# Row maxima in wider PSUM tiles: nine max items a pair instead of twelve, and none ahead of a score stretch

## The chip, the cores and the metric

One core of a Trainium2 chip runs the whole program in one launch. The metric is device time in microseconds (us) from the first to the last instruction and what lies around it, the median of several executions. The engines are named as in the profile: PE (TensorE matmul), PEld (its weight loads), DVE (VectorE), ACT (ScalarE), POOL (GpSimd), SP (SyncE, which issues the DMAs).

## What is computed

The reference, cut to its core: attention over keys with query rows pooled in twos, a soft mixture of experts over its rows, and a gated layer.

```python
def _attn_ref(q, k, v):                      # 4 x 8 heads, 1152 keys, 64 wide
    q_pool = q.reshape(B, H, S // 2, 2, D).mean(axis=3)      # 576 query rows a head
    scores = scale * np.matmul(q_pool, k.transpose(0, 1, 3, 2))
    scores = scores - np.max(scores, axis=-1, keepdims=True)
    attn = np.exp(scores)
    attn = attn / (np.sum(attn, axis=-1, keepdims=True) + 1e-09)
    return np.matmul(attn, v)

def _moe_ref(x, phi, w1, w2):                # 2304 rows, 8 experts with 4 slots each
    logits = x @ phi
    d = np.exp(logits - logits.max(0, keepdims=True))        # over the rows
    d /= d.sum(0, keepdims=True) + 1e-09
    ...                                      # slots, experts, combination

def _moe2_ref(x, w_gate, w_val, w_out, rms_g):   # RMS norm, silu gate, product
    ...
```

The part that the change touches is `np.max(scores, axis=-1)` of the attention, and the maximum over rows in `logits.max(0)`.

## The kernel before, in words

The 32 heads are taken as 16 pairs p; the two heads of a pair stand on partitions 0 to 63 and 64 to 127. For each pair there are nine key tiles `kt` of 128 keys and two halves `h` of 288 query rows. `qk` makes the scores of one (kt, h): four products for each head, the fourth of which subtracts the row maximum (`mr`), into a PSUM tile of two banks, one a head. ACT takes the exponential of it (`e`), POOL sums the exponentials (`add_e`, L395), and `av` multiplies them with the values (L401). `av` runs at every third key tile (`VISIT`), so that a third of a pair is: a stretch of six `qk` (48 score matmuls in the trace, 24 couples of one matmul a head), then a **visit** with the products with the values and all the small steps.

The row maximum must be there before the scores of a pair begin. It is made one pair ahead: a **max item** (`max_item`) multiplies 128 query rows of both heads with 384 keys (L327), and DVE reduces both banks in one instruction (L329). Twelve items, and two tail items for the last 64 query rows of both heads (L334, L335), make a pair's maxima. Then `max_red` (L340) takes the maximum over the key blocks, `max_row` turns it on PE (`mxt`, L345) and ACT copies it negated (`mrow`), and `send_row` sends it to `mr` by DMA.

The order of the work is written out by hand. `STEP` and `STEP_V` are the steps of one key tile; `m` marks where a max item may stand, `a b c` the three `av`. `MAX` gives the number of items that each key tile adds, and `AHEAD` how many items of the pair after next are made at a pair's end. `AT` gives each side step its moment: 5.75 is in key tile 5, at three quarters of its steps. In a visit stand also `sums`, `recips` and the two tail items (visit 1, key tile 2), `x_logits` (xl, L471) with `x_share` (L480) and `logit_add` (visit 2), and `x_turn` (xo, L453) with `x_divide` (xt, L462) (visit 3). In every fourth pair, `d_turn` (lgt, L508) turns the logits of a batch in visit 3 of the pair: six transposes into a tile of two banks, three a bank, and a maximum on DVE for each bank (mm, L509).

Scores, max items, xl, xo, lgt, sums and the other small results share one ring of three PSUM tiles of two banks (`tag="u", bufs=3`); whoever wants a tile waits until the engine that reads its former content is done:

```python
    def two_banks(name):
        return ps.tile([128, 2, 512], F32, tag="u", bufs=3, name=name)
```

After the last pair come the experts (hin, so), whose weights arrive by DMA, and the gated layer (yo, gv).

Of the kernel before, what the change touches and what calls it, by code (L numbers as in the profile page):

```python
# [15 lines left out]
AX = mybir.AxisListType  # L16
# [12 lines left out]
NF = 12  # L29

STEP = "q0 m q1 m e0 e1".split()
STEP_V = "q0 q1 m e0 e1 a m m b c m".split()
STEP_0 = "q m m e a b c".split()
VISIT = 3
PART = 5
MAX = [0, 0, 4, 0, 0, 4, 0, 0, 4]
MAX_1 = [2, 2, 4, 1, 0, 4, 0, 0, 4]
AHEAD = 5
AT = dict(
    take_x=0.0,  # L40
    load_64=[0.1, 3.0, 5.0],
# [3 lines left out]
    sum_q=2.2,  # L45
    round_k=[2.5, 5.5],
    abs_64=[2.51, 8.5, 8.51],
    d_back=2.68,
    d_copy=2.69,
    sums=2.7,  # L50
    max_tail=[2.75, 2.76],
    recips=2.77,
    turn_64=[0.5, 1.0, 3.3],
    low_q=3.2,
    high_q=5.51,
    block_q=5.52,
    max_red=5.65,
    slot_part=5.66,
    slot_copy=5.67,
    x_logits=5.7,  # L60
    max_row=5.83,
    send_row=6.0,
    x_share=6.05,
    logit_add=6.06,
    low_k=[6.1, 7.2],
    load_v=7.3,
    d_turn=8.66,
    slot_turn=8.67,
    x_turn=8.7,
    x_divide=[8.71, 8.72],  # L70
    drop_x=8.73,
    d_exp=8.85,
    c_soft=[3.5, 5.53, 8.96],
    load_ew=[1.0, 3.4],
# [39 lines left out]
    slot_part_a=8.2,  # L114
    slot_turn_a=9.43,
)
MAX_0 = [2, 1, 1, 1, 1, 1, 1, 1, 1, 1, 1, 2, 1, 1, 1, 1, 1, 0]
HALVED = (0, 15)
SQ_DVE = (0, 2)
SP_ACT = (1, 5, 4, 3, 2)  # L120
# [28 lines left out]
def attention_softmoe_gated_kernel(ctx: ExitStack, tc: tile.TileContext, kT, qT, vv, ip, cst, w1, w2, wg, wv, wo, rg, out):  # L149
# [78 lines left out]
    def two_banks(name):  # L228
        return ps.tile([128, 2, 512], F32, tag="u", bufs=3, name=name)
# [88 lines left out]
    def max_item(p, i):  # L318

        if i == 0:  # L320
            mx3[p] = S([128, 2 * NQT + 1, 3], "mx3")
        o = two_banks("mxp")
        if i < 12:
            t, c = divmod(i, 3)
            for s in range(2):
                r = slice(64 * s, 64 * s + 64)
                pe.matmul(o[:, s, 0:KC], lhsT=qh[p][r, 128 * t:128 * t + 128], rhs=kh[p][r, KC * c:KC * c + KC], start=True, stop=True)  # L327
            to = mx3[p][:, 0:2 * NQT].rearrange("p (s t) c -> p s t c", s=2)[:, :, t, c]
            dv.reduce_max(out=to, in_=o[:, :, 0:KC], axis=AX.X)  # L329
        else:  # L330
            n = 2 if i == 12 else 1
            for j in range(n):
                c = 2 * (i - 12) + j
                pe.matmul(o[:, j, 0:KC], lhsT=tb, rhs=kh[p][:, KC * c:KC * c + KC], start=True, stop=True)  # L334
            dv.reduce_max(out=mx3[p][:, 2 * NQT, 2 * (i - 12):2 * (i - 12) + n], in_=o[:, 0:n, 0:KC], axis=AX.X)  # L335

    rows = {}

# [160 lines left out]
    def d_turn(g):  # L499

        b, hs = groups[g]
        mm = S([32, 2], "mm")
        both = two_banks("lgt") if attention[0] else None
        o = []
        for i, h in enumerate(hs):
            o.append(both[0:32, i, 0:HQ] if attention[0] else bank([32, HQ], "lgt"))
            for t in range(3):
                pe.transpose(out=o[i][:, TB * t:TB * t + TB], in_=lg[b][:, 3 * h + t, :], identity=ident[0:TB, 0:TB])  # L508
            dv.reduce_max(out=mm[:, i:i + 1] if len(hs) > 1 else mall[:, g:g + 1], in_=o[i], axis=AX.X)  # L509
        if len(hs) > 1:  # L510
            dv.reduce_max(out=mall[:, g:g + 1], in_=mm, axis=AX.X)
        return o

    def d_neg(g):
# [177 lines left out]
    def side(p):  # L692
        n, m, l = p + 1, p + 2, p - 1
        todo = []

        def at(name, g):
            ts = (AT_0 if p == 0 else AT_15 if p == NP - 1 else AT).get(name, AT.get(name))
            for i, t in enumerate(ts if isinstance(ts, list) else [ts]):
                todo.append((t, len(todo), (lambda i=i: g(i))))

        if p == 0:
            at("round_k1", lambda i: round_k(1, i))
            at("block_q1", lambda i: block_q(1))
        if n < NP:
            at("low_k", lambda i: low_k(n, slice(576 * i, 576 * i + 576)))
            at("low_q", lambda i: low_q(n))
            at("load_v", lambda i: load_v(n))
            if p:
                at("max_tail", lambda i: max_item(n, 12 + i))
            at("max_red", lambda i: max_red(n))  # L710
            at("max_row", lambda i: max_row(n))
            at("send_row", lambda i: send_row(n))
        if m < NP:
            at("load_q", lambda i: load_q(m))
            at("load_k", lambda i: load_k(m))
            at("sum_q", lambda i: sum_q(m))
            at("high_q", lambda i: high_q(m))
            at("block_q", lambda i: block_q(m))
            at("round_k", lambda i: round_k(m, i))
        if l >= 0:  # L720
            at("take_x", lambda i: take_x(l))
            at("sums", lambda i: sums(l))
            at("recips", lambda i: recips(l))
            at("x_turn", lambda i: x_turn(l, range(3 * i, 3 * i + 3)) if p == NP - 1 else x_turn_all(l))
            at("x_divide", lambda i: x_divide(l, range(3 * i, 3 * i + 3)))
            at("drop_x", lambda i: rel("B"))
            at("x_logits", lambda i: x_logits(l, range(6)))
            at("x_share", lambda i: x_share(l, range(6)))
            at("logit_add", lambda i: logit_add(l))
            if p % 4 == 0 and p < NP - 1:  # L730
                at("d_turn", lambda i: dpart.__setitem__(("d", l // 4), (d_turn(l // 4), d_neg(l // 4))))
                at("d_exp", lambda i: d_exp(l // 4, *dpart.pop(("d", l // 4))))
            if p % 4 == 1 and p > 1:
                b = p // 4 - 1
                at("d_back", lambda i: d_back(b))
                at("d_copy", lambda i: d_copy(b))
                at("slot_part", lambda i: slot_part(b))
                at("slot_copy", lambda i: slot_copy(b))
                at("slot_turn", lambda i: slot_turn(b, pt[:, b]))
            if p % 4 == 2 and p > 2:  # L740
                b = p // 4 - 1
                at("c_soft", lambda i: (c_max, c_exp, c_soft2)[i](b))
        if 0 < p < NP - 2:
            at("load_64", lambda i: load_64() if i < 2 or p % 2 or p < 8 else None)
            at("load_ew", lambda i: load(1, 99, KEEP_C + min(len(doubles), 4 * HELD + HELD_O)) if p >= FIRST_EW else None)
        if p < NP - 1:
            at("spill", lambda i: spill())
            at("abs_64", lambda i: abs_64(1))
            at("turn_64", lambda i: turn_64(1))
        if p == NP - 2:  # L750
            spill()
            assert not doubles
            at("load_14", lambda i: (keep_b.__setitem__(0, KEEP[3]), load(1, KEEP_A[0])))
        if p == NP - 1:
            at("take_x_a", lambda i: take_x(p, (0,)))
            at("sums_a", lambda i: sums(p, (0,)))
            at("recips_a", lambda i: recips(p, (0,)))
            at("x_turn_a", lambda i: x_turn(p, ((0, 1), (2,))[i]))
            at("x_divide_a", lambda i: x_divide(p, ((0, 1), (2,))[i]))
            at("x_logits_a", lambda i: (x_logits(p, range(3)), x_share(p, range(3))))  # L760
            at("logit_add_a", lambda i: logit_add(p, (0,)))
            at("d_exp_a", lambda i: d_exp(3, d_turn(3), d_neg(3)))
            at("d_back_a", lambda i: (d_back(3), d_copy(3)))
            at("slot_part_a", lambda i: (slot_part(3), slot_copy(3)))
            at("slot_turn_a", lambda i: slot_turn(3, pt[:, 3]))
            at("load_15", lambda i: (keep_b.__setitem__(0, KEEP[0]), load(1, KEEP_A[1])))
        return sorted(todo, key=lambda x: x[:2])

    with tc.manual_schedule():
# [47 lines left out]
        def next_max(p, mx):  # L817
            if p == 0:
                mx += 9
                if mx < 14:  # L820
                    max_item(0, mx)
                    if mx == 13:
                        max_red(0)
                        max_row(0)
                        send_row(0, 3)
                else:
                    max_item(1, mx - 14)
            elif p == 1:
                max_item(2 + mx // 12, mx % 12)
            else:  # L830
                mx += AHEAD
                max_item(p + 1 + mx // 12, mx % 12)

        for p in range(NP):
            todo = side(p)
# [2 lines left out]
            for u, (kt, h) in enumerate(steps):  # L838
                now = u / 2 if p in HALVED else u
                order = STEP_0 if h is not None else STEP_V if kt % VISIT == VISIT - 1 else STEP  # L840
                quota = min(sum((MAX_0 if p == 0 else MAX_1 if p == 1 else MAX)[:u + 1]),
                            0 if p == NP - 1 else 12 - AHEAD if p == NP - 2 else 99)
                for i, step in enumerate(order):
                    while todo and todo[0][0] <= now + i / len(order) / len(steps) * 9:
                        todo.pop(0)[2]()
# [426 lines left out]
```

## Time and profile before

| | |
|---|---|
| time of three runs | 764.63, 765.6 and 769.43 us, median 765.6 |
| the profiled execution | 768.76 us, its span 766.7 us |
| PE busy | 726.6 us, 95% of the span |
| DVE, ACT, POOL busy | 61%, 52%, 59% |
| mean granted clock of TensorE | 0.987 |

The attention takes the first 510 us or so. Busy shares are averages over stages, and ends of matmuls are modelled, so that a busy PE may still lose time between matmuls; the starts of one stretch and of the next show it better.

### The profile page before, as it was taken

How to read it: one execution, taken by the hardware profiler on the slowest of the kernel's cores; microseconds unless marked ns; L12 is line 12 of the kernel's file. 1: busy time of each engine (PE TensorE's matmuls, PEld its weight loads, DVE VectorE, ACT ScalarE, POOL GpSimd, SP SyncE). 2: the span in 40 equal slices, each digit the busy share in tenths (PEclk: the TensorE clock that was granted, in tenths of full speed). 3: DMA queues.
4: the chain of work that ended last, by engine and by line, in shares of the span. 5: the costliest groups of instructions: out<-in, count | busy, mean ns of one | idle time of the engine just before them, and what ended most of it. 6: DMA issues, size and time to landing. Idle time of an engine off the chain costs nothing.

```text
span 766.7 us, 15557 instructions
## 1 busy us (share of the span) xinstructions
PE 726.6 (95%) x6143; PEld 503.5 (66%) x6143; DVE 468.0 (61%) x711; ACT 396.1 (52%) x809; POOL 448.5 (59%) x340
## 2 busy tenths in 40 slices
PE   4989999989999998999998999979989999999998
PEld 2556666656666665666666566644437788888887
DVE  5867877876688876678876665343134665545420
ACT  2455665655655654565565454343227775555330
POOL 5336887966768876778796577213005765535330
PEclk9999999999999999999999999997999999999999
DMA  4231452653625625445335053248994010000001
GB/s 168 93 110 54 174 177 88 226 190 125 215 95 208 212 74 204 141 145 191 127 132 199 6 169 125 100 165 311 377 382 167 1 56 28 15 27 29 29 27 42
DMA packets 52856, 103.57 MB, mean 135 GB/s; under 512 B 5816, under 2 KB 19632, under 8 KB 52784
## 3 DMA queue, kind: packets, MB, share of 16 engines
q1 hardware_dynamic: 52784, 102.59, 38.1%
q8 instruction: 48, 0.79, 0.4%
q14 instruction: 24, 0.20, 0.1%
HBM read 89.39 MB, written 13.11 MB: 134 GB/s over the span
## 4 chain that ended last, share of the span: by engine, by line
PE 82%; DVE 9%; ACT 4%; DMA 3%; issue 2%; POOL 1%; SPq 0%; ACTq 0%; DVEq 0%
PE yo L1175 19%; PE av L401 19%; PE sc L378 17%; PE mxp L327 5%; DVE mx L329 5%; PE gv L1127 3%; PE sums L421 2%; PE xl L471 2%; ACT e L380 2%; PE hin L944 2%; PE mxp L334 2%; DVE w L683 1%; PE xo L453 1%; PE so L967 1%; DMA w<-away 1%
## 5 line engine op out<-in xcount | busy, mean ns | idle before, releaser
L395 POOL TENSOR_TENSOR acc<-acc,e 128x576 f32<-128x576 f32 x148 | 215.2, 1481 | 60.9 <-ACT e L380 50.3
L380 ACT ACTIVATE e<-sc 128x576 f32<-128x576 f32 x288 | 170.2, 652 | 119.9 <-PE sc L378 118.0
L329 DVE TENSOR_REDUCE mx<-mxp 128x2 f32<-128x768 f32 x192 | 178.4, 955 | 87.7 <-PE mxp L327 86.1
L401 PE MATMUL av<-e,vt 128*64 128x288 f32 x1152 | 169.3, 425 | 0.0
L395 POOL TENSOR_TENSOR acc<-e 128x576 f32<-128x576 f32 x60 | 109.1, 1838 | 91.1 <-ACT e L380 91.1
L401 PEld LDWEIGHTS av<-e,vt 128*64 128x64 f32 x1152 | 74.5, 139 | 60.9 <-issue 26.6
L378 PE MATMUL sc<-qh,kh 64*128 64x288 f32 x576 | 95.8, 327 | 4.3 <-DVE mx L329 3.9
L1175 PE MATMUL yo<-woh,hA 128*128 128x512 f32 (+1 forms) x312 | 99.0, 384 | 0.0
L378 PE MATMUL sc<-mr,pick 64*128 64x288 f32 x576 | 86.4, 293 | 1.0 <-DMA mr<-mrow 1.0
L378 PE MATMUL sc<-qh,kl 64*128 64x288 f32 x576 | 85.9, 293 | 0.0
L378 PE MATMUL sc<-ql,kh 64*128 64x288 f32 x576 | 85.7, 292 | 0.0
L1132 DVE SCALAR_TENSOR_TENSOR th<-th,gv 128x384 f32<-128x384 f32 x72 | 39.9, 554 | 62.8 <-ACT th L1129 62.4
L327 PE MATMUL mxp<-kh,qh 64*128 64x384 f32 x384 | 70.7, 401 | 7.1 <-ACT kh L794 5.8
L1158 POOL TENSOR_TENSOR hA<-hu,hA 128x384 fp32r<-128x384 f32 x48 | 48.8, 1017 | 42.6 <-ACT hA L1157 38.8
L378 PEld LDWEIGHTS sc<-qh,kh 64*128 64x128 f32 x576 | 54.8, 185 | 27.5 <-DVE mx L329 16.2
L1175 PEld LDWEIGHTS yo<-woh,hA 128*128 128x128 f32 x312 | 57.6, 188 | 10.2 <-issue 0.7
L327 PEld LDWEIGHTS mxp<-kh,qh 64*128 64x128 f32 x384 | 34.1, 191 | 42.9 <-ACT e L380 16.3
L1175 PE MATMUL yo<-wol,hA 128*128 128x512 f32 (+1 forms) x151 | 57.8, 383 | 0.0
L1129 ACT ACTIVATE th<-gv 128x384 f32<-128x384 f32 x72 | 35.3, 490 | 42.4 <-PE gv L1127 39.1
L378 PEld LDWEIGHTS sc<-mr,pick 64*128 64x128 f32 x576 | 55.1, 185 | 1.4 <-DMA mr<-mrow 1.4
L378 PEld LDWEIGHTS sc<-qh,kl 64*128 64x128 f32 x576 | 55.5, 187 | 0.0
L378 PEld LDWEIGHTS sc<-ql,kh 64*128 64x128 f32 x576 | 55.0, 186 | 0.0
(180 smaller groups left out, 1038.4 us busy)
## 6 DMA issues: line engine op xcount, KB each, us to landing
w<-in_w_dram SPq DMA_DIRECT2D x86, 256.0 KB
w<-in_w_dram SPq DMA_DIRECT2D x21, 512.0 KB
vt<-in_vv_dram SPq DMA_DIRECT2D x16, 576.0 KB
qraw<-in_qT_dram SPq DMA_DIRECT2D x15, 576.0 KB
kraw<-in_kT_dram SPq DMA_DIRECT2D x15, 576.0 KB
away<-w SPq DMA_DIRECT2D x32, 256.0 KB
w<-away SPq DMA_DIRECT2D x32, 256.0 KB
raw<-in_wg_dram SPq DMA_DIRECT2D x12, 512.0 KB
```

The lines of the kernel that those rows point to most:

```text
L327: pe.matmul(o[:, s, 0:KC], lhsT=qh[p][r, 128 * t:128 * t + 128], rhs=kh[p][r, KC * c:KC * c + KC], start=True, stop=True)
L329: dv.reduce_max(out=to, in_=o[:, :, 0:KC], axis=AX.X)
L334: pe.matmul(o[:, j, 0:KC], lhsT=tb, rhs=kh[p][:, KC * c:KC * c + KC], start=True, stop=True)
L378: pe.matmul(o[:, s, 0:HQ], lhsT=w[r, wk], rhs=q[r, c], start=(i == 0), stop=(i == 3))
L380: ac.activation(ets[p, kt, h], o[:, :, 0:HQ], AF.Exp, scale=0.0625)
L395: eng.tensor_tensor(out=acc[p, h, j], in0=first[p, h, j] if n == 1 else acc[p, h, j], in1=e, op=ALU.add)
L401: pe.matmul(avt[p, h][64 * s:64 * s + 64, 0:HQ], lhsT=vt[p][:, kt, 64 * s:64 * s + 64], rhs=ets[p, kt, h][:, s], start=(kt == 0), stop=(kt ...
L1127: pe.matmul(o[i], lhsT=sg[n][:, 256 * i + 128 * c:256 * i + 128 * c + 128], rhs=cT[g], start=True, stop=True)
L1129: ac.activation(t, o[0], AF.Tanh, scale=0.5)
L1132: dv.scalar_tensor_tensor(out=t, in0=t, scalar=1.0, in1=o[0], op0=ALU.add, op1=ALU.mult)
L1158: gp.tensor_tensor(out=b, in0=u, in1=f(a), op=ALU.subtract)
L1175: pe.matmul(o, lhsT=x, rhs=w[:, c], start=(ft == 0 and i == 0), stop=(ft == NF - 1 and i == 2))
```

## The change

For pair 0 all stays as it was. From pair 1 on, a max item covers 512 keys and fills both its banks (L350 and L351 of the changed kernel): eight such items for keys 0 to 1023, and a ninth (L356, L357) that takes the last 128 keys for all four blocks of 128 query rows, in eight matmuls of 128 columns, with one reduction to eight columns. The two tail items take 2 x 512 and 128 keys. `MAX`, `MAX_1`, `MAX_0` and `AHEAD` follow (three items at each visit), and the last `m` of `STEP_V`, which put an item between a visit and the next stretch of scores, is gone. In `d_turn` the maxima of both banks are taken by one instruction after all six transposes. Side steps have new moments; of these `x_share` and `logit_add` go ahead of `max_row`, and `d_back` and `d_copy` behind `recips`.

```diff
-STEP_V = "q0 q1 m e0 e1 a m m b c m".split()
+STEP_V = "q0 q1 m e0 e1 a m m b c".split()
...
-MAX = [0, 0, 4, 0, 0, 4, 0, 0, 4]
-MAX_1 = [2, 2, 4, 1, 0, 4, 0, 0, 4]
-AHEAD = 5
+MAX = [0, 0, 3, 0, 0, 3, 0, 0, 3]
+MAX_1 = [1, 1, 3, 1, 0, 3, 0, 0, 3]
+NMAX = 9
+AHEAD = 3
...
-    x_share=6.05,
-    logit_add=6.06,
+    x_share=5.785,
+    logit_add=5.79,
...
         if i == 0:
             mx3[p] = S([128, 2 * NQT + 1, 3], "mx3")
+        if p:
+            return wide_item(p, i)
         o = two_banks("mxp")
...
+    def wide_item(p, i):
+
+        o = two_banks("mxp")
+        q, k, m = qh[p], kh[p], mx3[p]
+        heads = m[:, 0:2 * NQT].rearrange("p (s t) c -> p s t c", s=2)
+        rest = slice(1024, 1152)
+        if i < 8:
+            t, c = divmod(i, 2)
+            for s in range(2):
+                r = slice(64 * s, 64 * s + 64)
+                pe.matmul(o[:, s, :], lhsT=q[r, 128 * t:128 * t + 128], rhs=k[r, 512 * c:512 * c + 512], start=True, stop=True)
+            dv.reduce_max(out=heads[:, :, t, c], in_=o, axis=AX.X)
+        elif i == 8:
+            for t in range(NQT):
+                for s in range(2):
+                    r = slice(64 * s, 64 * s + 64)
+                    pe.matmul(o[:, s, 128 * t:128 * t + 128], lhsT=q[r, 128 * t:128 * t + 128], rhs=k[r, rest], start=True, stop=True)
+            dv.reduce_max(out=heads[:, :, :, 2], in_=o.rearrange("p s (t k) -> p s t k", t=NQT), axis=AX.X)
+        elif i == 9:
+            for c in range(2):
+                pe.matmul(o[:, c, :], lhsT=tb, rhs=k[:, 512 * c:512 * c + 512], start=True, stop=True)
+            dv.reduce_max(out=m[:, 2 * NQT, 0:2], in_=o, axis=AX.X)
+        else:
+            pe.matmul(o[:, 0, 0:128], lhsT=tb, rhs=k[:, rest], start=True, stop=True)
+            dv.reduce_max(out=m[:, 2 * NQT, 2:3], in_=o[:, 0:1, 0:128], axis=AX.X)
...
-            dv.reduce_max(out=mm[:, i:i + 1] if len(hs) > 1 else mall[:, g:g + 1], in_=o[i], axis=AX.X)
         if len(hs) > 1:
+            dv.reduce_max(out=mm, in_=both[0:32, :, 0:HQ], axis=AX.X)
             dv.reduce_max(out=mall[:, g:g + 1], in_=mm, axis=AX.X)
+        else:
+            dv.reduce_max(out=mall[:, g:g + 1], in_=o[0], axis=AX.X)
```

On PE, a plain pair's visit 2 and the begin of the next stretch of scores (mxp is a max item, sc a score) read before:

```order
L327 MATMUL mxp<-kh,qh 128x384 x2
L401 MATMUL av<-e,vt 64x288 x4
L327 MATMUL mxp<-kh,qh 128x384 x4
L471 MATMUL xl<-ipt,xu 96x64 x6
L401 MATMUL av<-e,vt 64x288 x8
L345 MATMUL mxt<-cs,mxw 128x128
L327 MATMUL mxp<-kh,qh 128x384 x2
L378 MATMUL sc<-qh,kh 128x288 x2
```

The same place in the changed kernel:

```order
L350 MATMUL mxp<-kh,qh 128x512 x2
L430 MATMUL av<-e,vt 64x288 x4
L350 MATMUL mxp<-kh,qh 128x512 x2
L356 MATMUL mxp<-kh,qh 128x128 x8
L500 MATMUL xl<-ipt,xu 96x64 x6
L430 MATMUL av<-e,vt 64x288 x8
L374 MATMUL mxt<-cs,mxw 128x128
L407 MATMUL sc<-qh,kh 128x288 x2
```

The max item ahead of the scores is gone, and the third item of this visit is the one of eight short matmuls.

On DVE, the reductions of the same visit with what stands before and behind them (w is the turning of 64-bit weights, ls and lg are `x_share` and `logit_add`), before:

```order
L329 TENSOR_REDUCE mx_1248<-mxp 128x2
L307 TENSOR_TENSOR ql<-qs,qh 128x576
L683 SCALAR_TENSOR_TENSOR w_1484<-w_1484,raw_1397 128x512
L329 TENSOR_REDUCE mx_1248<-mxp 128x2 x3
L340 TENSOR_REDUCE mxw<-mx_1248 128x9
L329 TENSOR_REDUCE mx_1652<-mxp 128x2
L480 TENSOR_TENSOR ls<-xl,rr 96x384
L490 TENSOR_TENSOR lg<-lg,ls 96x192
```

The same place in the changed kernel:

```order
L308 TENSOR_TENSOR ql<-qs,qh 128x576
L714 SCALAR_TENSOR_TENSOR w_1458<-w_1458,raw_1371 128x512
L351 TENSOR_REDUCE mx_1315<-mxp 128x2 x2
L357 TENSOR_REDUCE mx_1315<-mxp 128x8
L369 TENSOR_REDUCE mxw<-mx_1315 128x9
L509 TENSOR_TENSOR ls<-xl,rr 96x384
L519 TENSOR_TENSOR lg<-lg,ls 96x192
```

A reduction is gone ahead of ql and another ahead of ls.

On DVE, the maxima of the turned logits in every fourth pair, before:

```order
L329 TENSOR_REDUCE mx_2064<-mxp 128x2 x3
L509 TENSOR_REDUCE mm<-lgt 32x1 x2
L511 TENSOR_REDUCE mall<-mm 32x1
L516 TENSOR_SCALAR nm<-mall 32x1
L462 TENSOR_TENSOR xt<-xo,rr 96x3x128 x2
```

The same place in the changed kernel:

```order
L351 TENSOR_REDUCE mx_2119<-mxp 128x2 x3
L539 TENSOR_REDUCE mm<-lgt 32x2
L540 TENSOR_REDUCE mall<-mm 32x1
L547 TENSOR_SCALAR nm<-mall 32x1
L491 TENSOR_TENSOR xt<-xo,rr 96x3x128 x2
```

Two reductions, one a bank, have become one over both banks. The orders of SP and of POOL are the same in both kernels.

## Rows read from the trace of the kernel before

**Rows 1.** The page, part 1: engine, busy us, share of the span, instructions.

```profile
PE 726.6 (95%) x6143; PEld 503.5 (66%) x6143; DVE 468.0 (61%) x711; ACT 396.1 (52%) x809; POOL 448.5 (59%) x340
```

**Rows 2.** Waits of PE, 60 to 470 us: total us, times, longest.

```profile
PE lgt L508 <- DVE mm L509: 5.2, 3, 1.7
PE sc L378 <- DVE mx L329: 3.9, 14, 0.4
PE sums L421 <- DVE mx L329: 2.2, 3, 1.2
...
PE xl L471 <- DVE mx L329: 1.5, 3, 0.6
```

**Rows 3.** Timeline of PE, a plain pair's visits (start, us): item, scores, item.

```profile
252.70 0.44 PE L327 MATMUL mxp<-kh,qh 64*128 64x384 f32 x2
253.13 0.40 PE L378 MATMUL sc<-qh,kh 64*128 64x288 f32 x2
...
256.99 0.34 PE L327 MATMUL mxp<-kh,qh 64*128 64x384 f32 x2
...
259.71 2.16 PE L401 MATMUL av<-e,vt 128*64 128x288 f32 x16
261.80 0.44 PE L327 MATMUL mxp<-kh,qh 64*128 64x384 f32 x2
262.08 0.29 PE L378 MATMUL sc<-qh,kh 64*128 64x288 f32 x2
...
265.55 0.34 PE L327 MATMUL mxp<-kh,qh 64*128 64x384 f32 x2
```

**Rows 4.** Timeline of PE, pair 14: the one stretch without an item ahead of it.

```profile
468.15 0.40 PE L378 MATMUL sc<-qh,kh 64*128 64x288 f32 x2
...
471.34 0.29 PE L378 MATMUL sc<-mr,pick 64*128 64x288 f32 x2
471.56 1.19 PE L401 MATMUL av<-e,vt 128*64 128x288 f32 x8
```

**Rows 5.** Timeline of ACT in that stretch: six exponentials.

```profile
468.99 3.42 ACT L380 ACTIVATE e<-sc 128x576 f32<-128x576 f32 x6 [0.47 <-PE sc L378]
```

**Rows 6.** Groups by line and shape: count, busy us, mean ns of one.

```profile
L329 DVE TENSOR_REDUCE mx<-mxp 128x2 f32<-128x768 f32 x192 | 178.4, 955 | 87.7 <-PE mxp L327 86.1
...
L335 DVE TENSOR_REDUCE mx<-mxp 128x1 f32<-128x384 f32 x16 | 8.8, 549 | 0.4 <-PE mxp L334 0.4
```

**Rows 7.** The chain that ended last, 526 to 528 us: four matmuls of 96 columns.

```profile
526.79 0.62 PE c4o L988 x4
```

**Rows 8.** Timeline of PE around lgt in pair 4.

```profile
164.02 0.42 PE L508 MATMUL lgt<-cs,lg 96*32 96x96 f32 x3
...
166.19 0.42 PE L508 MATMUL lgt<-cs,lg 96*32 96x96 f32 x3 [1.74 <-DVE mm L509]
...
167.20 3.82 PE L401 MATMUL av<-e,vt 128*64 128x288 f32 x16
...
170.94 0.44 PE L327 MATMUL mxp<-kh,qh 64*128 64x384 f32 x2
```

**Rows 9.** Windows: from:to, length, busy of PE PEld DVE ACT POOL, PEclk, DMA share, GB/s.

```profile
120.40:148.80 28.40, 28.12 (x283) 19.28 (x285) 22.57 (x29) 17.69 (x33) 23.89 (x16) 1.00 0.54 184
...
167.20:170.90 3.70, 3.70 (x17) 1.71 (x16) 2.17 (x5) 1.46 (x5) 2.47 (x2) 0.54 0.82 318
490.00:500.00 10.00, 9.49 (x92) 5.93 (x88) 4.46 (x11) 3.45 (x7) 2.54 (x2) 1.00 0.00 0
510.00:580.00 70.00, 63.62 (x629) 30.90 (x630) 22.37 (x64) 22.66 (x57) 10.04 (x15) 0.93 0.96 349
```

**Rows 10.** Timeline of DVE and PE around visit 2 of a plain pair.

```profile
272.36 0.96 DVE L329 TENSOR_REDUCE mx<-mxp 128x2 f32<-128x768 f32 x1 [0.24 <-PE mxp L327]
...
279.34 0.18 DVE L340 TENSOR_REDUCE mxw<-mx 128x9 f32<-128x27 f32 x1
...
280.79 0.33 PE L345 MATMUL mxt<-cs,mxw 128*128 128x128 f32 x1
```

More of the change, by code (lines that the diff above doesn't have):

```diff
@@ L47 @@
     abs_64=[2.51, 8.5, 8.51],
[L48 to L52, printed above, removed]
+    sums=2.75,
+    max_tail=[2.85, 2.86],
+    recips=2.87,
+    d_back=2.88,
+    d_copy=2.89,
     turn_64=[0.5, 1.0, 3.3],
@@ L56 @@
     block_q=5.52,
[L57 to L61, printed above, removed]
+    max_red=5.75,
+    slot_part=5.76,
+    slot_copy=5.77,
+    x_logits=5.78,
+    x_share=5.785,
+    logit_add=5.79,
+    max_row=5.95,
     send_row=6.0,
-    x_share=6.05,
-    logit_add=6.06,
     low_k=[6.1, 7.2],
     load_v=7.3,
[L67 to L71, printed above, removed]
+    d_turn=8.73,
+    slot_turn=8.74,
+    x_turn=8.75,
+    x_divide=[8.76, 8.77],
+    drop_x=8.78,
     d_exp=8.85,
@@ L116 @@
 )
-MAX_0 = [2, 1, 1, 1, 1, 1, 1, 1, 1, 1, 1, 2, 1, 1, 1, 1, 1, 0]
+MAX_0 = [2, 1, 1, 1, 1, 0, 1, 1, 1, 1, 1, 1, 1, 1, 1, 1, 0, 0]
 HALVED = (0, 15)
@@ L708, in side @@
             if p:
-                at("max_tail", lambda i: max_item(n, 12 + i))
+                at("max_tail", lambda i: max_item(n, NMAX + i))
             at("max_red", lambda i: max_red(n))
@@ L828, in next_max @@
             elif p == 1:
-                max_item(2 + mx // 12, mx % 12)
+                max_item(2 + mx // NMAX, mx % NMAX)
             else:
                 mx += AHEAD
-                max_item(p + 1 + mx // 12, mx % 12)
+                max_item(p + 1 + mx // NMAX, mx % NMAX)
         for p in range(NP):
@@ L841, in attention_softmoe_gated_kernel @@
                 quota = min(sum((MAX_0 if p == 0 else MAX_1 if p == 1 else MAX)[:u + 1]),
-                            0 if p == NP - 1 else 12 - AHEAD if p == NP - 2 else 99)
+                            0 if p == NP - 1 else NMAX - AHEAD if p == NP - 2 else 99)
                 for i, step in enumerate(order):
```

## The prediction

> **What bounds the kernel now.** I read the shares of the page first, then the waits, then the timeline of PE. PE is busy 95% of the span and DVE 61% [rows 1], so the attention is bound by PE, and only what takes time from PE's own row counts. The waits name four places where PE waits for a reduction of DVE: the second bank of lgt (5.2 us in 3 waits), scores (3.9 in 14), sums (2.2) and xl (1.5) [rows 2]. That list undercounts: a wait that falls into the modelled tail of a matmul isn't in it. So I measure stretches from start to start. The reader is to see in the timeline of a plain pair that an item stands ahead of each stretch of scores (252.70 to 253.13, 0.43 us; 261.80 to 262.08, 0.28), and that the stretch behind it lasts 3.86 us in one case and 3.47 in the other [rows 3], for the same 24 couples of matmuls. One stretch of the trace, in pair 14, has no item ahead: 468.15 to 471.56, 3.41 us with the changeover to av in it [rows 4]. Its last couple takes 0.22 us to that changeover and the other 23 take 3.19, or 0.139 each; so a stretch that goes on into an item, as the others do, would last 24 x 0.139 = 3.33 us. The rest of 3.86 and 3.47 is waiting: with three tiles in the ring, the third scores want the tile that the item ahead of them still holds until DVE has read it.
>
> A plain pair takes about 28.4 us, with PE counted busy for 28.1 of it; POOL is busy for 23.9, DVE 22.6, ACT 17.7 [rows 9].
>
> **The item ahead of the scores.** Removed, three times a pair. The stretch behind visit 2 (253.13) has the longer wait, the two others are like 262.08. In scores a pair gives back (3.86 - 3.33) + 2 x (3.47 - 3.33) = 0.81 us. The three items themselves, with their share of switching and waiting, take 0.43 + 2 x 0.28 = 0.99 us. Together 1.80 us a pair. I take the full 0.99, since the first scores behind av pay for their own weight loads in pair 14 too (they are inside the 3.41).
>
> **Wider items.** The columns stay: 12 x 384 = 8 x 512 + 4 x 128 for each head. So what the items ahead streamed comes back as longer items: at 2.4 GHz 384 columns are 0.16 us, 128 more are 0.053, and eight items carry them: 0.43 us a pair. The two tail items keep their columns and count: nothing.
>
> The ninth item is the unknown: eight matmuls of 128 columns, each with its own weight load. If they ran at the pace of the score columns, four couples would take 4 x 0.139 x 128/288 = 0.25 us. The nearest row of short matmuls behind full weight loads is c4o: four of 96 columns in 0.62 us, changeover included, 0.155 each [rows 7]. Eight of these one after another would be 1.24 us. Scores show that the matmuls of the two heads run side by side (two weight loads and two matmuls in 0.139 us), so I take four couples at a little under the pace of c4o, 0.48 us. Against the 0.16 us of the item it replaces that is 0.32 more, with ends at 0.09 and 1.08.
>
> A plain pair thus gains 1.80 - 0.43 - 0.32 = **1.05 us** (ends 0.29 and 1.28). Pairs 2 to 14 have this pattern: 13 x 1.05 = **13.7 us** (3.8 to 16.6).
>
> **The maximum of the turned logits.** In pairs 4, 8 and 12 the second three transposes begin 2.17 us after the first (164.02 to 166.19), waiting 1.74 us for the maximum of the first bank; then av, which lasts 2.09 us in a plain pair (259.71 to 261.80 [rows 3]), lasts 3.74 (167.20 to 170.94 [rows 8]). In that stretch the granted clock is 0.54, nearly all at the lower of the two levels, 1.2 GHz, after PE had stood still for lgt; in the plain pair it is 1.00 [rows 9]. The three transposes themselves take about 0.26 us, so the visit loses 1.9 us to the wait and 1.65 to the clock, 3.55 in all. With one reduction behind all six transposes PE goes on. What is late next is xo, which follows and wants the tile of the second item; its reduction can't end before two reductions after the first item, and I leave 0.5 us for that. Whether so short a stop brings the clock down, no row here shows; I take it that it doesn't, and let the low end pay the 1.65 us again. So 3.0 us an occasion, **9.0 us** (1.4 to 3.55 each, 4 to 11).
>
> **Waits of sums and xl.** Six visits lose 3.7 us because DVE has weights to turn or a softmax to finish ahead of the first item's reduction [rows 2]. The change takes a reduction of 0.96 us out of DVE's queue ahead of that, as at 272.36 [rows 10], but a reduction of 1024 elements holds longer: 549 ns for 384 and 955 for 768 [rows 6] give 1.06 ns an element, so 1.23 us, 0.27 more. Net 0.69 us less for each visit: **3 us** of the 3.7 (0 to 3.7).
>
> **Pair 1**, where items also stand between scores, has five fewer: 1.5 us (0 to 3). Pair 0 keeps its own items; its items for pair 1 are fewer and longer on DVE in proportion: 0.
>
> **Moved steps.** `x_share` and `logit_add` run on DVE at most 1 us earlier, ahead of the turned row's copy, which ACT makes; this frees xl's tile for the second scores, and DVE's 5.8 idle microseconds of a plain pair [rows 9] hide it; without them it would delay scores by its own length. `d_back` goes behind `recips`, three times, with the same six transposes: there it waits for a tail item's tile, here it stood ahead of `sums`; I take nothing, and bound it by half of a reduction, 0.6 us each way. SP and POOL keep their order, so each load follows the same PE event as before.
>
> **The sum.** 13.7 + 9.0 + 3 + 1.5 = 27 us. The profiled execution, 768.76 us, would become 741.5; it stands 3.2 us above the median, and the median 765.6 becomes **739**.
>
> **Rival 1: longer reductions hold their tiles too long, or eight short matmuls are dear.** An item's tile is held 0.27 us longer, and in each visit the third user behind the first item (xl, xo, sums) takes that tile. If each of them waited the whole of it, 13 x 3 x 0.27 = 10.5 us would be lost: 750. A ninth item at its dear end costs 13 x 0.76 = 10 us: also 750. For the first speaks nothing in a plain pair: the user comes after av and two more items, some 1.9 us behind the first item's start, and the reduction would be done 0.4 + 1.23 us after it. The Trainium skill, in "Perfetto Trace Analysis", section "Optimizing Scalar/DVE Operations", speaks for this rival: where VectorE isn't saturated but causes bubbles on another engine, it advises to break instructions up, and the change does the opposite. By that rule the time would be the 750 above; the trace agrees with its premise (61% busy, and the bubbles), while no row here shows a longer reduction's effect.
>
> **Rival 2: ACT becomes the bound of the stretch.** Six exponentials take 3.42 us [rows 5] against 3.33 for a stretch. They can run on into the visit, and in pair 14 they kept up without an item ahead, so it has little for it. If each of the 38 stretches lost 0.3 us, 11 us would go: 750 as well. A case like rival 1.
>
> **Rival 3: the gain stays in the attention.** From 510 to 580 us the DMA engines are busy 0.96 of the time, with the experts' weights. If these came no earlier, only the idle 0.04 of these 70 us could be saved, 3 us: 763. Against it: from 490 to 500 the DMA share is 0.00 [rows 9], so the loads wait for room that PE frees, and the whole stretch shifts with the attention's end.
>
> **Rival 4, slower.** In visit 2, mxt waits for `max_red`, which stands behind three reductions, now 0.8 us longer in sum. Before, `max_red` ends at 279.52 and mxt starts at 280.79, 1.27 us later [rows 10]. Should DVE fall behind by that and 2 us more in every pair, PE would stand as long as it does at lgt, the clock would come down, and a pair would lose 2 + 1.65 us: 13 x 3.65 = 47 us against the 27 gained, 786. It decides from about 2.1 us a pair (27/13). Against it: DVE has a reduction fewer to do both before and after, and 5.8 idle microseconds a pair.
>
> **How the numbers follow.** Forecast 739, with its terms off by a quarter either way 732 to 746: 0.70. Rivals 1 and 2, 746 to 753: 0.19. Rival 3, about 763: 0.08. Rival 4: 0.03. The range is 732 to 751, into rivals 1 and 2. A change within 1% (758 to 773) is about what a measurement of this kernel can't tell from none. Faster 0.89, same 0.08, slower 0.03. That the change doesn't do what it says is no case of its own: the orders of PE and DVE show the items gone.
>
> **What would show it.** In the changed kernel's trace: stretches of scores of 3.3 us behind av; a plain pair of 27.3 us; the ninth item at about 0.5 us of PE; reductions of 1.2 us; lgt without a wait of its own, with av behind it at 2.1 us and the clock at 1.00; sums and xl with under 1 us of waits. Wrong would be a new wait of PE for a reduction (xo, mxt), scores that wait for exponentials, or an expert stretch that begins earlier and ends no earlier.

## The result, and the profile after

The changed kernel takes 745.08 us in the median (743.92 to 745.67 in four runs) against 766.7 of the kernel before beside it: a ratio of 0.971 with an interval of 0.968 to 0.975, 2.9% faster. The forecast was 739 with a range of 732 to 751. The profiled execution of the changed kernel stands at 744.83 us (span 742.8), so at its median, where that of before, 768.76 (span 766.7), stood above its own. The spans differ by 23.9 us; the terms of the forecast add up to 27.

The page of the changed kernel, part 1, and then its waits of PE from 60 to 470 us (total us, times, longest), to be held against [rows 1, 2]:

```profile
PE 710.6 (96%) x6143; PEld 500.3 (67%) x6143; DVE 426.6 (57%) x663; ACT 391.7 (53%) x809; POOL 423.3 (57%) x340
```

```profile
PE xo L482 <- DVE mx L351: 3.0, 6, 0.5
PE dn L565 <- DVE mx L361: 2.8, 3, 0.9
PE sums L450 <- POOL acc L424: 0.7, 1, 0.7
PE xl L500 <- DVE xt L491: 0.4, 1, 0.4
```

All four waits of before are off the list, but for one wait of 0.3 us of xl in pair 1; the two of sums and xl that are listed have other releasers and belong to pair 15, where the kernel before has them too, behind 470 us. No scores wait for a reduction any more. In their place stand two smaller ones: xo, which is the 0.5 us that the forecast left at lgt, three times, and as much again behind the transposes of `slot_turn` (pto) in three other pairs; and dn, 0.93 us three times, which the forecast had at nothing.

The timeline of PE in a plain pair of the changed kernel (start, us, form), the counterpart of [rows 3]:

```profile
237.19 0.50 PE L350 MATMUL mxp<-kh,qh 64*128 64x512 f32 x2
237.52 0.56 PE L356 MATMUL mxp<-kh,qh 64*128 64x128 f32 x8
238.01 1.23 PE L500 MATMUL xl<-ipt,xu 128*96 128x64 f32 x12
...
241.52 0.40 PE L407 MATMUL sc<-qh,kh 64*128 64x288 f32 x2
...
244.85 0.39 PE L350 MATMUL mxp<-kh,qh 64*128 64x512 f32 x2
...
247.74 2.16 PE L430 MATMUL av<-e,vt 128*64 128x288 f32 x16
249.83 0.40 PE L407 MATMUL sc<-qh,kh 64*128 64x288 f32 x2
...
253.18 0.41 PE L350 MATMUL mxp<-kh,qh 64*128 64x512 f32 x2
```

Scores begin right behind mxt or av, and the stretches last 241.52 to 244.85 = 3.33 us and 249.83 to 253.18 = 3.35, against 3.86 and 3.47 before; the last two av take 2.09 (247.74 to 249.83), as before. The ninth item takes 0.49 us (237.52 to 238.01). A plain pair from start to start is the first of these windows (from:to, length, busy of PE PEld DVE ACT POOL, PEclk, DMA share, GB/s), 27.32 us against the 28.40 of [rows 9], which is 28.36 from the start of one stretch to the next (120.54 to 148.90); the second holds the visit with lgt:

```profile
117.60:144.92 27.32, 27.32 (x284) 19.16 (x282) 18.48 (x27) 17.42 (x33) 21.94 (x15) 1.00 0.56 191
158.00:163.50 5.50, 5.01 (x40) 2.68 (x36) 5.11 (x8) 3.32 (x8) 5.50 (x5) 1.00 0.85 261
```

That visit on PE's timeline, for [rows 8], and the reductions of the items, for [rows 6] (count, busy us, mean ns of one, idle before):

```profile
159.47 0.67 PE L537 MATMUL lgt<-cs,lg 96*32 96x96 f32 x6
160.63 0.86 PE L482 MATMUL xo<-cs,xu 128*96 128x128 f32 x6 [0.49 <-DVE mx L351]
161.42 2.16 PE L430 MATMUL av<-e,vt 128*64 128x288 f32 x16
163.51 0.40 PE L407 MATMUL sc<-qh,kh 64*128 64x288 f32 x2
```

```profile
L351 DVE TENSOR_REDUCE mx<-mxp 128x2 f32<-128x1024 f32 x120 | 144.3, 1223 | 110.2 <-PE mxp L350 110.1
...
L357 DVE TENSOR_REDUCE mx<-mxp 128x8 f32<-128x1024 f32 x15 | 18.2, 1215 | 0.0
```

All six transposes run at once, xo waits 0.49 us behind them, the granted clock stays at 1.00 and av lasts 2.09 us instead of 3.74. A wide reduction takes 1.22 us.

**Where the 23.9 us come from.** I laid the starts of the stretches of both traces side by side. The 38 plain thirds of pairs 2 to 14 give 12.5 us (1.04 a pair); the three thirds with lgt give another 8.6 beside that (2.87 each); the waits of sums and xl 3.7; pairs 0 and 1 1.3. Together 26.1. Taken back are 1.2 at dn, 0.6 behind pto (0.2 us three times) and 0.4 in the experts and the gated layer. The 1.3 of pairs 0 and 1 isn't clear of chance: pair 2 begins at 81.69 us in the trace of before and at 83.56 in that of e1, whose pairs 0 and 1 are the same, and at 80.43 to 82.25 in four traces with the changed kernel's pairs 0 and 1 (its own, e2, e6, e9).

### The profile page after: what moved, and what is told of

Same layout as the page of the kernel before. It is cut to its first block, busy times and chain, and to the rows that moved or that the text cites. A ratio compares the mean times of both kernels' runs of the same rounds, so it can differ in the third digit from the quotient of the medians.

```text
span 742.8 us, 15502 instructions
## 1 busy us (share of the span) xinstructions
PE 710.6 (96%) x6143; PEld 500.3 (67%) x6143; DVE 426.6 (57%) x663; ACT 391.7 (53%) x809; POOL 423.3 (57%) x340
## 4 chain that ended last, share of the span: by engine, by line
PE 88%; DVE 5%; DMA 3%; issue 2%; ACT 1%; POOL 1%; SPq 0%; ACTq 0%; DVEq 0%
PE sc L407 21%; PE av L430 20%; PE yo L1206 20%; PE mxp L350 5%; PE gv L1158 3%; PE sums L450 2%; PE xl L500 2%; PE hin L975 2%; DVE mx L351 2%; PE xo L482 1%; PE so L998 1%; DMA w<-away 1%; PE mxp L360 1%; PE pp L580 1%; DMA w<-in_w_dram 1%
## 5 line engine op out<-in xcount | busy, mean ns | idle before, releaser
L409 ACT ACTIVATE e<-sc 128x576 f32<-128x576 f32 x288 | 165.7, 658 | 95.4 <-PE sc L407 93.6
L351 DVE TENSOR_REDUCE mx<-mxp 128x2 f32<-128x1024 f32 x120 | 144.3, 1223 | 110.2 <-PE mxp L350 110.1
L430 PE MATMUL av<-e,vt 128*64 128x288 f32 x1152 | 164.7, 416 | 0.0
L424 POOL TENSOR_TENSOR acc<-e 128x576 f32<-128x576 f32 x60 | 84.7, 1432 | 89.6 <-ACT e L409 89.6
L430 PEld LDWEIGHTS av<-e,vt 128*64 128x64 f32 x1152 | 72.6, 136 | 60.1 <-issue 24.1
L407 PE MATMUL sc<-ql,kh 64*128 64x288 f32 x576 | 87.2, 294 | 0.0
L350 PE MATMUL mxp<-kh,qh 64*128 64x512 f32 x240 | 48.6, 435 | 0.0
L1165 DVE SCALAR_TENSOR_TENSOR hu<-th,gv 128x384 f32<-128x384 f32 x72 | 39.9, 554 | 8.4 <-DVE th L1163 0.5
```

The source lines that it names most:

```text
L350: pe.matmul(o[:, s, :], lhsT=q[r, 128 * t:128 * t + 128], rhs=k[r, 512 * c:512 * c + 512], start=True, stop=True)
L351: dv.reduce_max(out=heads[:, :, t, c], in_=o, axis=AX.X)
L407: pe.matmul(o[:, s, 0:HQ], lhsT=w[r, wk], rhs=q[r, c], start=(i == 0), stop=(i == 3))
L409: ac.activation(ets[p, kt, h], o[:, :, 0:HQ], AF.Exp, scale=0.0625)
L424: eng.tensor_tensor(out=acc[p, h, j], in0=first[p, h, j] if n == 1 else acc[p, h, j], in1=e, op=ALU.add)
L430: pe.matmul(avt[p, h][64 * s:64 * s + 64, 0:HQ], lhsT=vt[p][:, kt, 64 * s:64 * s + 64], rhs=ets[p, kt, h][:, s], start=(kt == 0), stop=(kt ...
```

## The experiments

The median of each kernel is compared with runs of the kernel before on the same chip. The experiments ran on three chips, so where two of them, or one and the changed kernel, are held against each other by their times, a difference of a microsecond or two is read from the traces.

**e1: the kernel before with the new maximum of the turned logits alone.**

```diff
-            dv.reduce_max(out=mm[:, i:i + 1] if len(hs) > 1 else mall[:, g:g + 1], in_=o[i], axis=AX.X)
         if len(hs) > 1:
+            dv.reduce_max(out=mm, in_=both[0:32, :, 0:HQ], axis=AX.X)
...
```

> The kernel before with the new maximum of the turned logits alone. Theory (each wait of lgt costs the wait and, through the clock, the av behind it): three occasions of 2.9 us, the time falls by about 8.6 us against the profiled run of before, to 757 to 761; lgt lasts 1.2 us with the wait of xo in it, av behind it 2.09 us, and the clock stays at 1.00 there. Rival (the wait only moves to xo or to the exponentials of the logits, and the clock falls as before): under 3 us.

Measured: 761.4 us (759.97 to 761.7) against 767.0 (764.35 to 770.93), ratio 0.991 (0.988 to 0.995): small, but clear of noise, and 0.4 us above what was expected. At lgt xo waits 0.28 us, and av lasts 2.09 us in all three visits, at a granted clock of 1.00. The first of them as a window:

```profile
167.60:169.69 2.09, 2.09 (x17) 1.07 (x16) 1.88 (x6) 0.95 (x4) 2.09 (x2) 1.00 1.07 428
```

5.6 us come from this part in the median. What stands out is the spread: six runs within 1.7 us, where 15 of before lie 6.6 apart. Of those 15, the six at 764.4 to 764.9 have a mean granted clock of 0.991 to 0.993 and the one at 770.93 has 0.982. So the clock's part of the gain is paid in some runs of before and not in others, and against its quickest runs this part is worth some 3 us.

**e2: the changed kernel with the old maxima, one a bank** (the diff of e1 the other way round).

> The changed kernel with the old maxima of the turned logits, one a bank. Theory (the two parts add up): 8 to 9 us slower than the changed kernel, 752 to 754, some 13 to 15 us under before; stretches of scores still 3.33 us, lgt near 2.4 us and av behind it 3.7 us. Rival (what the items gain already hides the wait of lgt): within 3 us of the changed kernel.

Measured: 752.97 us (752.64 to 757.66), ratio 0.982 (0.977 to 0.987); 7.9 us above the changed kernel. Its timeline shows two of the three occasions, and the windows the av behind them:

```profile
163.89 0.42 PE L537 MATMUL lgt<-cs,lg 96*32 96x96 f32 x3 [2.21 <-DVE mm L538]
...
164.90 3.85 PE L430 MATMUL av<-e,vt 128*64 128x288 f32 x16
...
282.01 0.42 PE L537 MATMUL lgt<-cs,lg 96*32 96x96 f32 x3 [2.22 <-DVE mm L538]
...
283.02 2.16 PE L430 MATMUL av<-e,vt 128*64 128x288 f32 x16
```

```profile
164.90:168.60 3.70, 3.70 (x17) 1.66 (x16) 2.50 (x7) 1.46 (x5) 0.79 (x1) 0.54 1.00 392
283.20:285.20 2.00, 2.00 (x18) 0.97 (x16) 1.72 (x5) 1.46 (x5) 0.59 (x1) 1.00 1.02 413
```

The wait is the same, 2.21 and 2.22 us; behind the first the clock is 0.54 and av lasts 3.85, behind the second it is 1.00 and av lasts 2.16 (both with the modelled end). The third is like the second, so the expected av of 3.7 us came at one occasion of three. Over the profiles of five kernels that have this wait (before, e2, e3, e4, e8) the clock came down at 9 of 15 occasions; behind lgt in the others (after, e1, e5, e6, e7, e9) at none. What decides between the two isn't seen in these rows, so the clock term was a chance and not a price. The wait itself is 1.66 to 1.74 us in the three kernels with narrow items and 2.21 to 2.29 in the two with wide ones, where the maximum of the first bank stands behind wider reductions. Whether the part is worth more in the changed kernel (7.9 us) than in the one before (5.6) stays open: 1.8 of the 7.9 lie ahead of pair 2 in the two profiles, where the kernels are the same.

**e3: placing alone.** The kernel before with its twelve narrow items; the fourth of a visit goes between av b and av c, so that none stands ahead of scores.

```diff
-STEP_V = "q0 q1 m e0 e1 a m m b c m".split()
+STEP_V = "q0 q1 m e0 e1 a m m b m c".split()
...
-    max_row=5.83,
+    max_row=5.95,
...
-    d_exp=8.85,
+    d_exp=8.95,
```

> The kernel before with its twelve narrow items, but the fourth of each visit between two av and none ahead of the scores (the turned row and the exponentials of the logits a little later, so that they stay behind the last av). Theory (the place of the item makes the scores wait, not its width): stretches of scores 3.33 us in place of 3.45 to 3.86, so 0.8 us a pair; the item now costs a change of array shape on both sides, about 0.1 us more each; 5 to 10 us under before. Rival (the gain is in fewer and wider items and in DVE's saved instructions): no change beyond 2 us.

Measured: 768.18 us (765.81 to 770.98, ten runs), ratio 1.002 (0.999 to 1.004): no gain, and a miss for my theory, by which no item ahead of scores should have given 5 to 10 us. The timeline of a visit 1, and the longest of PE's waits from 60 to 470 us, show where it stays:

```profile
139.60 0.40 PE L378 MATMUL sc<-qh,kh 64*128 64x288 f32 x2
...
142.95 0.35 PE L327 MATMUL mxp<-kh,qh 64*128 64x384 f32 x2
...
148.80 0.44 PE L327 MATMUL mxp<-kh,qh 64*128 64x384 f32 x2 [0.55 <-DVE mx L335]
149.17 1.19 PE L401 MATMUL av<-e,vt 128*64 128x288 f32 x8
```

```profile
PE mxp L327 <- DVE mx L335: 7.7, 14, 0.6
```

The stretch is short as expected, 3.35 us. But the item that was moved now waits 0.55 us for a tail item's tile, 14 times, 7.7 us in all, and takes 0.37 (148.80 to 149.17) where it stands. A pair lasts 28.64 us. The third of a pair that ends in visit 1 is 0.62 us longer than before (10.69 against 10.07), the two others are 0.02 and 0.31 shorter. In those the item waits for nothing, but between two av it costs some 0.1 to 0.25 us more than it did ahead of the scores, which eats part of what the scores gain. I had to replace the theory: what a visit can take without waiting is set by the three tiles of the ring, and a fourth item is one user too many where a visit has several others. If so, the same item directly behind the third must make those behind it wait (e8), and fewer, wider items must be what makes room (e4, e2).

**e8: placing alone, at the other place**, the fourth item right behind the third. The moments of the side steps follow, as `sums` 2.7 to 2.75, `max_red` 5.65 to 5.75, `max_row` 5.83 to 5.95, `d_turn` 8.66 to 8.74, `d_exp` 8.85 to 8.95.

```diff
-STEP_V = "q0 q1 m e0 e1 a m m b c m".split()
+STEP_V = "q0 q1 m e0 e1 a m m m b c".split()
```

> The kernel before with its twelve narrow items, the fourth of each visit directly behind the third, so that no change of array shape is added, and none ahead of the scores. Theory (placement needs a free tile of the ring, which the wide items give and a fourth narrow item takes): stretches of scores 3.33 us, but xl, xo and sums now follow as the second user behind the second item, whose reduction ends some 0.7 us later than they come; three such waits a pair eat the 0.8 us of the scores and the 0.5 us of the item: 0 to 10 us slower than before. Rival (placement alone is enough where it adds no change of shape): 1.3 us a pair, 12 to 20 us faster.

Measured: 780.53 us (780.03 to 780.98), ratio 1.015 (1.012 to 1.017), 11.6 us slower and a little more than expected. Its timeline at a visit 3:

```profile
135.07 0.40 PE L378 MATMUL sc<-qh,kh 64*128 64x288 f32 x2
...
138.40 0.34 PE L327 MATMUL mxp<-kh,qh 64*128 64x384 f32 x2
...
139.78 0.79 PE L327 MATMUL mxp<-kh,qh 64*128 64x384 f32 x6
141.28 0.86 PE L453 MATMUL xo<-cs,xu 128*96 128x128 f32 x6 [0.71 <-DVE mx L329]
```

Again 3.33 us for the stretch, but xo is the fourth user behind the first item, wants the second item's tile and waits 0.71 us for its reduction; the three items with this take 1.50. In the changed kernel xo is the third user behind the first item, and in a plain pair its tile has been read by then.

**e4: width alone.** The kernel before with the nine wide items, of which one still stands ahead of each stretch: `wide_item` as in the change, the old logits and the old moments.

```diff
-STEP_V = "q0 q1 m e0 e1 a m m b c m".split()
+STEP_V = "q0 q1 n e0 e1 a m m b c m".split()
...
-MAX = [0, 0, 4, 0, 0, 4, 0, 0, 4]
-MAX_1 = [2, 2, 4, 1, 0, 4, 0, 0, 4]
-AHEAD = 5
+MAX = [0, 0, 3, 0, 0, 3, 0, 0, 3]
+MAX_1 = [2, 1, 3, 1, 0, 3, 0, 0, 3]
+NMAX = 9
+AHEAD = 4
```

(`n` does nothing.)

> The kernel before with the nine wide items, one of them still ahead of each stretch of scores, and the old moments and logits. Theory (the tile of the item ahead is held until its reduction is done, now 1.23 us and not 0.96): the scores wait 0.27 us longer in each stretch, which with the longer items takes back what three fewer items give; 0 to 10 us slower than before. Rival (fewer items and fewer DVE instructions are the gain): 8 to 13 us faster than before.

Measured: 780.17 us (779.27 to 781.27), ratio 1.016 (1.012 to 1.020), 13 us slower, which is the expected direction and more than the 10 us at most. The waits of PE, 60 to 470 us:

```profile
PE sc L407 <- DVE mx L351: 15.0, 39, 0.6
```

Before these were 3.9 us in 14 waits [rows 2]. The item ahead of scores holds its tile for 1.22 us instead of 0.96, and the third scores want it: stretches of 3.82 to 4.28 us.

With the old logits throughout this makes a square: narrow with an item ahead (before) 766.7 to 768.9; narrow without 768.2 or 780.5, by where the fourth item goes (e3, e8); wide with one ahead (e4) 780.2; wide without (e2) 753.0. The place alone gives nothing or costs 12 us, the width alone costs 13, both together give 14 (767.0 to 753.0 on one chip). The gain is in neither; the waits in the traces put it in three items a visit and none ahead of the scores, for a ring of three tiles, which needs both. One impurity stays: e2 has the changed kernel's moments of side steps, e4 those of before, e3 and e8 their own. What the moments alone are worth was not tried.

**e5: the changed kernel with each wide item's reduction split in two**, one a bank.

```diff
-            dv.reduce_max(out=heads[:, :, t, c], in_=o, axis=AX.X)
+            for s in range(2):
+                dv.reduce_max(out=heads[:, s, t, c:c + 1], in_=o[:, s, :], axis=AX.X)
```

> The changed kernel with the reduction of each of the eight wide items split in two, one a bank (the advice to break up instructions of an engine that isn't saturated but holds up another). Theory (the tile comes free at the second half's end, and PE isn't waiting for these reductions in a plain pair): DVE's busy time grows by 13 pairs x 8 x 0.15 = 16 us, the time by 0 to 3 us. Rival (the advice holds here, shorter reductions let PE go on earlier): 3 us or more faster.

Measured: 745.91 us (745.46 to 746.51), ratio to before 0.972 (0.967 to 0.976), so 0.8 us above the changed kernel, of which its trace has 0.5 in pairs 2 to 14. Its group of reductions:

```profile
L352 DVE TENSOR_REDUCE mx<-mxp 128x1 f32<-128x512 f32 x240 | 151.7, 685 | 106.5 <-PE mxp L350 106.5
```

Two instructions of 685 ns for one of 1223 hold the tile a little longer, not shorter, as both banks are one tile: 1.26 us of DVE's time an item (151.7 us for 120) instead of 1.20 (144.3). The Trainium skill, "Perfetto Trace Analysis", section "Optimizing Scalar/DVE Operations", says that breaking instructions up may let work finish sooner where VectorE isn't saturated but makes bubbles on other engines. It gave nothing here, but the test is a weak one: in the changed kernel few bubbles are left behind these reductions (xo, 3.0 us in six waits, and 3.4 in this run), and two halves of one tile free it no earlier.

**e7: how near rival 1 was.** The changed kernel with the reduction of each visit's first item made twice.

```diff
-            dv.reduce_max(out=heads[:, :, t, c], in_=o, axis=AX.X)
+            for _ in range(2 if i in (0, 3, 6) else 1):
+                dv.reduce_max(out=heads[:, :, t, c], in_=o, axis=AX.X)
```

> The changed kernel with the reduction of the first item of each visit done twice (the same result), so that its tile is held 1.15 us longer. Theory (there is about 0.5 us of slack between that reduction's end and the third user of its tile): sums, xl and xo then wait 0.5 to 0.7 us each, 1.9 us a pair, 20 to 27 us in all. Rival (DVE is idle a fifth of the time, so a longer reduction costs nothing): within 3 us of the changed kernel.

Measured: 784.25 us in the one run that was made, 39 above the changed kernel and more than expected. The waits of PE, 60 to 470 us:

```profile
PE sums L451 <- DVE mx L352: 11.6, 13, 0.9
PE xo L483 <- DVE mx L352: 8.6, 13, 0.9
PE xl L501 <- DVE mx L352: 8.3, 10, 1.7
```

Of the 1.15 us added ahead of the other reductions, 0.77 to 0.95 show up in each third of a plain pair, in these waits and in the items. So the slack behind the first reduction is 0.2 to 0.4 us. The change used up 0.27 of what there was, and rival 1 missed by that little. The length of a reduction thus counts as soon as this slack is used up.

**e6: the changed kernel with three side steps later**, to get back what dn and pto lost.

```diff
-    d_back=2.88,
-    d_copy=2.89,
+    d_back=2.95,
+    d_copy=2.96,
...
-    slot_turn=8.74,
+    slot_turn=8.85,
```

> The changed kernel with d_back and d_copy behind the last av of visit 1 and slot_turn between the last two av of visit 3. Theory (the transposes of d_back wait 1.0 us for a tail item's tile three times, those of slot_turn's followers 0.2 us): 3 to 3.6 us faster than the changed kernel, 741 to 742. Rival (the wait moves to the first scores behind them): same within 1 us.

Measured: 741.04 us (740.22 to 741.78), ratio to before 0.965 (0.962 to 0.968), 4.0 below the changed kernel: the best of all. The place of dn in pair 4, in the changed kernel and then here:

```profile
171.84 0.49 PE L459 MATMUL sumt<-cs,srow 128*96 128x128 f32 x3
173.26 0.47 PE L565 MATMUL dn<-cs,dtx 32*96 32x32 f32 x6 [0.93 <-DVE mx L361]
```

```profile
172.98 0.49 PE L459 MATMUL sumt<-cs,srow 128*96 128x128 f32 x3
173.40 1.19 PE L430 MATMUL av<-e,vt 128*64 128x288 f32 x8
174.52 0.47 PE L565 MATMUL dn<-cs,dtx 32*96 32x32 f32 x6
```

One av between sumt and dn covers the reduction of the tail item, and the wait is gone, 2.8 us in three; pto gives the rest.

**e9: e6 with the turning of the logits later too.**

```diff
-    d_turn=8.73,
+    d_turn=8.84,
...
-    d_exp=8.85,
+    d_exp=8.95,
```

> The kernel with the later steps (d_back, d_copy, slot_turn) and d_turn between the last two av of visit 3 too, its exponentials behind the last av. Theory (xo then comes as in other pairs, lgt finds its tile free, but its tile is held by the exponentials until after the second scores): the 0.5 us wait of xo goes, a wait of the scores of 0 to 0.7 us comes, three times: between 1.5 us faster and 1 us slower than the kernel with the later steps, 739.5 to 742. Rival (the wait of xo just goes): 1.5 us faster or more.

Measured: 742.84 us (742.76 to 744.6), ratio 0.966 (0.964 to 0.968), 1.8 above e6 and outside what was expected. The two ran on different chips; in the traces pairs 2 to 14 take 2.4 us more than in e6. The waits of PE, 60 to 470 us:

```profile
PE sc L407 <- ACT dtx L557: 1.3, 3, 0.4
...
PE sc L407 <- ACT e L409: 1.0, 3, 0.3
```

xo no longer waits at lgt, but the exponentials of the logits (dtx) now meet those of the scores on ACT, and the stretch behind lasts 4.58 us instead of 3.33. A wait of 0.5 us was traded for 1.25.

## Why the prediction was right, and where its numbers were off

- **The item ahead of the scores, the wider items.** Right, and nearly to the number: stretches of 3.33 (forecast 3.33), the ninth item 0.49 (0.48, a choice between 0.25 and 1.24, so with some luck), reductions of 1.22 (1.23), a plain pair 1.04 us shorter (1.05). In the whole 12.5 instead of 13.7, since pairs 2 to 14 hold 38 plain thirds, not 39, and one of them grew by 0.2. That neither edit gains anything without the other (e3, e4, e8) the prediction didn't see: it added 0.99 for the items and 0.81 for the scores as if each stood by itself.
- **The maximum of the turned logits.** 2.87 us an occasion in the profiled pair (forecast 3.0), 8.6 in all. The mechanism held: no wait at the second bank, 0.49 us at xo (0.5), av at full clock. But the 1.65 us of the clock were taken as sure on the side of before. e2 shows the same wait with and without the fall, 9 falls in 15, and the profiled execution of before had all three.
- **Waits of sums and xl.** 3.7 us gone, forecast 3, but not by the reduction alone. In these visits the turning of weights or the end of a softmax, which stand in DVE's queue ahead of the first item's reduction, also became shorter, which the forecast didn't have. One wait of xl, before, then the same place in the changed kernel:

```profile
215.24 1.92 DVE L683 SCALAR_TENSOR_TENSOR w<-w,raw 128x512 uint32<-128x512 uint32 x1
219.57 1.23 PE L471 MATMUL xl<-ipt,xu 128*96 128x64 f32 x12 [0.62 <-DVE mx L329]
```

```profile
205.97 0.68 DVE L714 SCALAR_TENSOR_TENSOR w<-w,raw 128x512 uint32<-128x512 uint32 x1
208.87 1.23 DVE L351 TENSOR_REDUCE mx<-mxp 128x2 f32<-128x1024 f32 x1 [0.44 <-PE mxp L350]
```

DVE is idle for 0.44 us before that reduction, but w is 1.24 us shorter. With w as long as before, the reduction would have come 0.8 us later, more than the slack of 0.2 to 0.4 (e7). By such numbers, over the five visits whose waits went, some 1.5 of the 3.7 us hang on the shorter instructions; that is an estimate.

- **Pair 1**: 1.3 with pair 0, forecast 1.5; two traces of one code differ by more than that in this place, so it is no test of the term.
- **Moved steps.** This is the term that failed. `d_back` behind the tail items was put at nothing, with 0.6 us as the bound; dn waits 0.93 us for a tail item's reduction each time, 2.8 us. Before, `sums` waited for ACT's copy of dn, 1.6 us in three, which is gone, so 1.2 us are the loss. `slot_turn` wasn't weighed at all and lost 0.6. Moving both by a few steps gave 4.0 us (e6).
- **The sum.** 23.9 us of span instead of 27: half of the miss of 6. The other half is the 3.2 us by which the profiled execution of before stood above its median; I carried it over whole, and the changed kernel's stands at its median. The runs of before with a mean clock of 0.991 or more lie mostly at 764 to 766 us and those at 0.982 at 770.7 to 771, so it fits that a good part of that offset was the clock behind lgt, which is gone with the wait.
- **Rival 1** didn't happen: 0.2 to 0.4 us of slack were left in a plain pair (e7). **Rival 2** didn't: 3.33 us a stretch. **Rival 3** didn't: from pair 14's stretch without an item, at 443.83 us of the changed kernel and 468.15 of before [rows 4], to the end of the span it is 299.0 against 298.6 us, so all the time gained by then arrives, less 0.4. **Rival 4** didn't: mxt doesn't wait. The start of pair 14's stretch in the changed kernel:

```profile
443.83 0.40 PE L407 MATMUL sc<-qh,kh 64*128 64x288 f32 x2
```

## What to carry to other kernels

Where several kinds of results share a small ring of tiles, count the users between a tile's writing and its next use, and the time its reader needs, before moving or widening any of them: two edits that alone gave nothing or cost 12 to 13 us gave 14 together, because only both brought the items of a visit down to what three tiles carry. A step that is moved behind such a user inherits its reader's time, and one piece of other work between the two hides it. And an execution that stands off its median may owe that to something the change removes; then the offset isn't carried over.

## What the runs showed of the hardware that was not expected

The same wait of 2.2 us brought TensorE's granted clock down to 0.54 for the 3.7 us of the next av in one place and left it at 1.00 in another of the same execution (e2).

VectorE and GpSimd instructions that the change doesn't touch became much shorter. The turning of weights on DVE and the first sum of exponentials on POOL, in the kernel before:

```profile
L683 DVE SCALAR_TENSOR_TENSOR w<-w,raw 128x512 uint32<-128x512 uint32 x36 | 48.0, 1354 | 0.0
```

```profile
L395 POOL TENSOR_TENSOR acc<-e 128x576 f32<-128x576 f32 x60 | 109.1, 1838 | 91.1 <-ACT e L380 91.1
```

and in the changed kernel:

```profile
L714 DVE SCALAR_TENSOR_TENSOR w<-w,raw 128x512 uint32<-128x512 uint32 x36 | 28.1, 801 | 0.0
```

```profile
L424 POOL TENSOR_TENSOR acc<-e 128x576 f32<-128x576 f32 x60 | 84.7, 1432 | 89.6 <-ACT e L409 89.6
```

The same count and shape, 1354 against 801 ns and 1838 against 1432. Of the 41.4 us by which DVE's busy time fell [rows 1], the weights are 19.9 and the maxima, over all their groups, about 5. The traces show when these instructions are long. In the two, all 26 turnings beside which no POOL instruction ran took 673 to 685 ns, and all 23 that took over 1.7 us (19 before, 4 in the changed kernel) ran beside a sum on POOL. All 86 first sums beside which DVE ran no instruction with two tensor operands took 1.41 to 1.44 us; all 30 that took over 1.5 us, up to 2.93, had one beside them. So these instructions are long only where both engines run them at the same moment, and the changed kernel's order brings them together less often. It isn't the width of the items: in e8, with narrow ones, a turning takes 786 ns. No run changed this meeting alone, and why it makes them longer stays open. Most of the shorter time lies where PE doesn't wait for it; the part behind sums and xl, about 1.5 of the 23.9 us by the estimate above, does count.
